# Scores of three more batches as plain float32 products, and fewer operations on GpSimd, in a fused attention and mixer kernel

## The chip, the cores and the metric

The kernel runs on one core of a Trainium2 chip. The metric is the device time of one execution in microseconds (us); lower is better. The engines are named as in the profile: PE (TensorE, matrix products), PEld (its weight loads), DVE (VectorE), ACT (ScalarE), POOL (GpSimd) and SP (SyncE, which issues all DMAs here).

## The reference, cut to what matters

```python
def _attn_ref(q, k, v):                      # 8 batches, 8 heads, 576 positions, 64 wide
    scores = np.matmul(q, k.transpose(0, 1, 3, 2)) / np.sqrt(64)
    scores = np.where(block_i >= block_j, scores, -1e9)      # blocks of 64 positions
    scores = scores - np.max(scores, axis=-1, keepdims=True)
    attn = np.exp(scores)
    attn = attn / (np.sum(attn, axis=-1, keepdims=True) + 1e-09)
    return np.matmul(attn, v)

def _moe_ref(x, w_theta, w_tok_r, w_tok_i, w_ch):            # x: 8 x 576 x 512
    theta = x @ w_theta
    zr, zi = x * np.cos(theta), x * np.sin(theta)
    y = np.einsum('ts,bsd->btd', w_tok_r, zr) + np.einsum('ts,bsd->btd', w_tok_i, zi)
    u = x + y
    return u + np.maximum(u @ w_ch, 0.0)
```

The output of the attention, with the heads side by side, is the x of the second function.

## The kernel before, in words

Every batch b has four pairs of heads, so that pairs p run from 0 to 31 and heads n from 0 to 63. A pair goes through these steps. q and k arrive by DMA, 128 rows (two heads of 64) by 640 columns. `scores` multiplies them in three pieces, "ab", "c" and (in `first_scores`) "d". `maxima` takes the row maxima on DVE, five pieces (L588), and `exponentials` takes exp on ACT out of PSUM into a tile t (L592). `high` writes 2^15 t in float16 (L314 to L320, a helper `times` that all such casts share), `low` on DVE writes what float16 lost (L619), a DMA transposes both (L623), `weighted` multiplies them with v on PE (L638), and `normalise` divides (L645 to L653).

When the four pairs of a batch are there, the mixer of that batch follows: `theta` (PE, L727) in five blocks of rows i = 0 to 4; `turns` (ACT, L737) and `rest` (DVE, L743) reduce the angle; `size` and `sines` (ACT, L749 to L763) give cosine and sine; `times_x` ("z", L773), `z_high` ("zh") and `z_low` ("zl", L786) make the operand and its two float16 parts; `mix` (PE, L796) sums over positions in steps n = 0 to 4, and step n needs the z parts of step n; `take_u` (L809), `u_high`, `u_low` (L820), `channel` (PE, L828) and `rectify` (L834) finish, and the result is stored. The x parts (`x_high`, `x_low`, L713), the sums `add_parts` ("xs", L801) and `unscale` ("xd") stand between the attention and the mixer.

A product of float32 numbers is made in two ways. In a *split* product each operand is cut into a high and a low part, and three fast products are summed: high with high, low with high, high with low. For the scores the parts are `q_high`, `q_low` (L519), `k_high` and `k_low` (L524) in the type float32r. In a *plain* product the float32 operands go to PE as they are. The constant `PLAIN = 4` says that pairs 0 to 3 take the plain way, in the scores and also in everything up to `weighted`: for them t is turned on PE (`turn_half`, L604) rather than by DMA.

Nothing in the kernel loops over time: all steps are put into one table of parts, each with what it needs, and `PLACES` gives the place of each part in one long order. Each engine, and SP's queue, runs its own steps in that order and no other, so that a step that waits holds up everything behind it on its engine. `BANKS` gives the PSUM bank of each result, `RUNNING` puts matmuls that compute nothing at some places (L1032), and `ON` says for each kind of step and each instance which engine runs it: P is POOL, D is DVE, A is ACT.

```python
products = [(hi, pair.v1), (hi, pair.v2), (lo, pair.v1)]                 # weighted, split
return (self.qh, self.kh), (self.ql, self.kh), (self.qh, self.kl)       # scores, split
return (self.qh, self.k),                                                # scores, plain
needs = [("mix", b, dt, th, n - 1)] if n else ...                        # order within mix
```

Of the kernel before, what the change touches and what calls it, by code (L numbers as in the profile page):

```python
# [180 lines left out]


RUNNING = [
    (12, 0, 7), (24, 0, 12), (41, 0, 8), (53, 0, 1), (74, 0, 2), (334, 7, 12), (354, 0, 3)
]
ON = {"w5": "APAAAAA",
      "wc": "DPPDDD",
      "vc": "PDPPDDPDPPPPDDDPDPPPDPPP",
      "qh": "PPPAPPPPPAAAPAAAAAPPPAAPAPPPAAPP",
      "vf": "PPPP",  # L190
      "cp": "AADDDAAADAADADDA",
# [14 lines left out]
PLAIN = 4  # L206
# [879 lines left out]
```

## Time and profile before

| | |
|---|---|
| median of 3 runs | 690.64 us (688.83 to 692.03) |
| the profiled execution, own time | 691.77 us |
| its span, first to last instruction | 690.0 us |
| busy: PE, PEld | 660.6 us (96%), 537.5 us (78%) |
| busy: DVE, ACT, POOL | 587.2 us (85%), 482.1 us (70%), 308.3 us (45%) |
| share of the span on the chain that ended last | PE 57%, DVE 20%, DMA 9%, ACT 8%, issue 4%, POOL 1% |

A busy share is a mean over stages with different limits. The chain that ended last follows the work back from the last instruction, each time to what released it. An engine's idle time counts only where that engine, or one that waits for it, sets the end. In a timeline, matmuls overlap, so the time that PE needs for a group is taken from the start of the group to the start of the next.

### The profile page before, as it was taken

How to read it: one execution, taken by the hardware profiler on the slowest of the kernel's cores; microseconds unless marked ns; L12 is line 12 of the kernel's file. 1: busy time of each engine (PE TensorE's matmuls, PEld its weight loads, DVE VectorE, ACT ScalarE, POOL GpSimd, SP SyncE). 2: the span in 40 equal slices, each digit the busy share in tenths (PEclk: the TensorE clock that was granted, in tenths of full speed). 3: DMA queues.
4: the chain of work that ended last, by engine and by line, in shares of the span. 5: the costliest groups of instructions: out<-in, count | busy, mean ns of one | idle time of the engine just before them, and what ended most of it. 6: DMA issues, size and time to landing. Idle time of an engine off the chain costs nothing.

```text
span 690.0 us, 17713 instructions
## 1 busy us (share of the span) xinstructions
PE 660.6 (96%) x7427; PEld 537.5 (78%) x7427; DVE 587.2 (85%) x846; ACT 482.1 (70%) x746; POOL 308.3 (45%) x280
## 2 busy tenths in 40 slices
PE   7998999999979999999999999999999999999997
PEld 4787866789657769887787768888797878888677
DVE  5897998998989999998979899999998999865342
ACT  4998699667896688877876598757867659613420
POOL 1513545422333734553653244674472673825640
PEclk9997999999989999999999999999999999999999
DMA  9971279699799888699866897969996875650001
GB/s 329 344 259 54 80 162 172 133 187 190 201 168 185 177 200 172 162 190 207 197 155 136 172 182 158 204 140 184 193 214 116 150 130 124 134 108 35 35 1 69
DMA packets 245855, 110.52 MB, mean 160 GB/s; under 512 B 227216, under 2 KB 227216, under 8 KB 245776
## 3 DMA queue, kind: packets, MB, share of 16 engines
q1 hardware_dynamic: 245776, 109.40, 71.5%
q8 instruction: 58, 0.95, 0.6%
q14 instruction: 21, 0.17, 0.1%
HBM read 43.06 MB, written 9.44 MB: 76 GB/s over the span
## 4 chain that ended last, share of the span: by engine, by line
PE 57%; DVE 20%; DMA 9%; ACT 8%; issue 4%; POOL 1%; SPq 0%; ACTq 0%; DVEq 0%; POOLq 0%
PE ps L796 20%; PE ps L828 11%; PE ps L727 10%; PE ps L638 8%; PE ps L554 7%; DVE m L588 4%; DMA pt<-p 3%; DVE p L619 3%; ACT t L592 2%; DMA q<-in_qT 2%; DVE zl L786 2%; DVE u_all L809 1%; ACT p L316 1%; DMA w_raw<-in_w_tok 1%; DMA raw_v<-in_v 1%
## 5 line engine op out<-in xcount | busy, mean ns | idle before, releaser
L592 ACT ACTIVATE t<-ps,m 128x576 f32<-128x576 f32 (+4 forms) x320 | 148.4, 528 | 59.1 <-DVE m L588 47.7
L796 PE MATMUL ps<-wT_h,zh 128*128 128x288 f16 x540 | 155.5, 288 | 5.9 <-ACT zh L314 3.0
L796 PE MATMUL ps<-wT_h,zl 128*128 128x288 f16 x540 | 155.2, 287 | 1.8 <-DVE zl L786 1.8
L796 PE MATMUL ps<-wT_l,zh 128*128 128x288 f16 x540 | 155.2, 287 | 0.0
L588 DVE TENSOR_REDUCE m<-ps 128x2 f32<-128x640 f32 (+4 forms) x160 | 125.7, 814 | 11.9 <-PE ps L559 9.7
L796 PEld LDWEIGHTS <-zh 128*128 128x128 f16 x1080 | 106.0, 98 | 30.9 <-ACT zh L314 3.1
L638 PE MATMUL ps<-v,pt 128*128 128x65 f16 (+1 forms) x2760 | 117.4, 202 | 7.0 <-DMA pt<-p 4.6
L619 DVE SCALAR_TENSOR_TENSOR p<-t,p 128x1664 f16<-128x1664 f32 x56 | 110.5, 1976 | 8.5 <-ACT p L316 7.2
L638 PEld LDWEIGHTS <-pt 128*128 128x128 f16 x2520 | 81.8, 97 | 10.8 <-DMA pt<-p 5.9
L727 PE MATMUL ps<-wth_h,xt 128*128 128x512 f16 (+1 forms) x384 | 87.6, 345 | 0.2 <-DVE xt L713 0.2
L727 PEld LDWEIGHTS <-xt 128*128 128x128 f16 (+1 forms) x576 | 45.9, 102 | 43.3 <-issue 1.6
L828 PE MATMUL ps<-uh,wch_h 128*128 128x288 f32 x256 | 78.5, 307 | 0.5 <-DVE u_all L834 0.4
L828 PE MATMUL ps<-ul,wch_h 128*128 128x288 f32 x256 | 75.6, 295 | 0.0
L828 PE MATMUL ps<-uh,wch_l 128*128 128x288 f32 x256 | 75.6, 295 | 0.0
L316 ACT ACTIVATE p<-t 128x1664 f16<-128x1664 f32 x47 | 74.6, 1590 | 1.0
L796 PEld LDWEIGHTS <-zl 128*128 128x128 f16 x540 | 53.1, 98 | 19.0 <-issue 3.0
L727 PE MATMUL ps<-wth_l,xt 128*128 128x512 f16 (+1 forms) x192 | 57.3, 343 | 0.0
L554 PE MATMUL ps<-kh,qh 64*128 64x288 f32 (+1 forms) x336 | 53.9, 312 | 1.9 <-ACT t L592 1.6
L828 PEld LDWEIGHTS ps<-uh,wch_h 128*128 128x128 f32 x256 | 48.1, 188 | 2.4 <-DVE u_all L834 1.0
L554 PE MATMUL ps<-kh,ql 64*128 64x288 f32 (+1 forms) x336 | 48.9, 284 | 0.0
L554 PE MATMUL ps<-kl,qh 64*128 64x288 f32 (+1 forms) x336 | 48.7, 283 | 0.0
L828 PEld LDWEIGHTS ps<-ul,wch_h 128*128 128x128 f32 x256 | 48.1, 188 | 0.1
(154 smaller groups left out, 1345.4 us busy)
## 6 DMA issues: line engine op xcount, KB each, us to landing
raw_v<-in_v SPq DMA_DIRECT2D x32, 384.0 KB, 4.4
q<-in_qT SPq DMA_DIRECT2D x32, 320.0 KB, 3.3
k<-in_kT SPq DMA_DIRECT2D x32, 320.0 KB, 3.5
out<-u_all SPq DMA_DIRECT2D x32, 288.0 KB, 2.2
w_raw<-in_w_tok SPq DMA_DIRECT2D x9, 576.0 KB, 5.8
w_raw<-in_w_theta SPq DMA_DIRECT2D x4, 512.0 KB, 7.5
w_raw<-in_w_ch SPq DMA_DIRECT2D x4, 512.0 KB, 4.9
pt<-p SPq DMA_TRANSPOSE x56, 6.2
```

The source lines that it names most:

```text
L316: engine.mul(to, x, scale)
L554: nc.tensor.matmul(s[hh][:, col:col + n], lhsT=qq[rows, i * P:(i + 1) * P], rhs=kk[rows, k0:k0 + n], start=nn == 0 and (j == 0 or c == "ab ...
L588: nc.vector.tensor_reduce(out=m, in_=s, axis=AX.XY if i in (2, 3) else AX.X, op=ALU.max, negate=True)
L592: nc.scalar.activation(out=to, in_=s, func=AF.Exp, scale=1.0, bias=m)
L619: nc.vector.scalar_tensor_tensor(out=self.p[:, 1, :], in0=self.t, scalar=LIFT, in1=self.p[:, 0, :], op0=ALU.mult, op1=ALU.subtract)
L638: nc.tensor.matmul(o[:, i, :], lhsT=pp[:, block, :], rhs=vv[:, of, hh, :], start=nn == 0, stop=nn == n - 1)
L727: nc.tensor.matmul(g[rows, 0:cols.stop - cols.start], lhsT=x[:, dt, part, i, rows], rhs=ww[:, dt, cols], start=(n == 0), stop=(n == 11))
L786: engine_of("zl", (2 * self.b + hf) * 5 + n).tensor_tensor(out=zl, in0=cv, in1=zh, op=ALU.subtract)
L796: nc.tensor.matmul(g, lhsT=zz[:, kk, cols], rhs=ww[:, kk, ts], start=(n == 0 and kk == k0 and nn == 0), stop=(n == 4 and nn == 2))
L809: nc.vector.scalar_tensor_tensor(out=self.u(dt)[:, ts], in0=bank("y", self.b, dt, th)[:, 0:HS], scalar=self.batch.unit, in1=self.u(dt)[:, ...
L828: nc.tensor.matmul(g[:, 0:HS], lhsT=ww[:, dt, e * P:(e + 1) * P], rhs=uu[:, dt, th * HS:(th + 1) * HS], start=(n == 0), stop=(n == 11))
```

## The change

`PLAIN` is split in two. A new `WHOLE = 4` keeps the old boundary for everything after the scores, and `PLAIN = 16` now governs the scores alone: pairs 4 to 15 (batches 1 to 3) have plain scores, their k goes by DMA straight to where PE reads it, and their steps `k_high`, `k_low` and `q_low` are gone. In `ON` the kinds v1, high, xh, xl, zh, kl, xs, xd and uh have no P any more. `PLACES`, `BANKS` and `RUNNING` are new throughout, as the list of parts is shorter (2570 for 2606); the filling matmuls are 45 in both.

```diff
-    3, 2, 17, 20, 23, 63, 101, 118, 8, 6, 34, 37, 39, 52, 102, 138, 27, 30, 72, 77, 79, 137, 228, 248, 47, 44, 85,
...
 RUNNING = [
-    (12, 0, 7), (24, 0, 12), (41, 0, 8), (53, 0, 1), (74, 0, 2), (334, 7, 12), (354, 0, 3)
+    (12, 0, 7), (25, 0, 13), (44, 0, 8), (64, 0, 3), (314, 0, 4), (370, 3, 5), (376, 3, 2), (386, 3, 3)
 ]
-      "kh": "DDDDPAPPAAPPAAPAPAAPPAAPPAPPAAPP",
-      "kl": "DDDDDPPPDDPDDPPDDDDPDDDDDPPPDPDP",
-      "v1": "DDDDPAPAPAPAAPAAAAAPAPPAAAAAAPAP",
-      "high": "DDDDDDDDAAPAAAAAAAAAAAAAAAAPAAAAAAAAPAAAAAAAPAAAAAAAPPAAAAPPAPAA",
-      "xh": "AAAAAAAAPDAAAADPAPADAAPPDPAPADPPAADPAPA",
-      "xl": "DDDDDPPDPDPDPDDDDPDDDDDPDPPDPDPPDPDDDDD",
-      "zh": "APDPPDAADPAPDDPADAPDADADDAPAAAAADAAAAAADAAAAPDDADAAPAADAPDAAPPAAADDAAPPDPAAPPDPA",
-      "xs": "DDDDPDDPDPDPPDPD",
-      "xd": "DAPPAAAADAAAPADA",
-      "uh": "AAAPAAAAAPAAAPAA",
+      "v1": "DDDDAAAAAAAAAAAAAAAAAAAAAAAAAAAA",
+      "high": "DDDDDDDDAAAAAAAAAAAAAAAAAAAAAAAAAAAAAAAAAAAAAAAAAAAAAAAAAAAAAAAA",
+      "kh": "DDDDDDDDDDDDDDDDAAPPAAPAAPPPAAPP",
+      "kl": "DDDDDDDDDDDDDDDDDDDDDDDDDDDDDDDD",
+      "xh": "AAAAAAAAADAAAADAAAADAAAADAAAADAAAADAAAA",
+      "xl": "DDDDDDDDDDDDDDDDDDDDDDDDDDDDDDDDDDDDDDD",
+      "zh": "AAAAAAAAAAAAAAAAAAAAAAAAAAAAAAAAAAAAAAAAAAAAAAAAAAAAAAAAAAAAAAAAAAAAAAAAAAAAAAAA",
+      "xs": "DDDDDDDDDDDDDDDD",
+      "xd": "DDDDAAADDAAADAAA",
+      "uh": "AAAAAAAAAAAAAAAA",
...
-PLAIN = 4
+WHOLE = 4
+PLAIN = 16
...
-            if pair.p < PLAIN:
+            if pair.p < WHOLE:
                 products = [(self.turned.rearrange("p a c q -> p (a c q)").bitcast(F32).rearrange("p (c q) -> p c q", q=P), pair.whole)]
...
-            if p < PLAIN:
+            if p < WHOLE:
                 free_pt = turn_of(f"pt{hh}", [("weighted", n)])
```

Three places show what moves. All line numbers of the changed kernel are one lower than before.

PE, the scores of pair 9 (batch 2), pieces "d" and "c", with the matmuls that add the mask. k and q are the operands, h and l their high and low parts. Before:

```order
L567 MATMUL ps<-kh,qh 128x64 x2
L567 MATMUL ps<-kh,ql 128x64 x2
L567 MATMUL ps<-kl,qh 128x64 x2
L554 MATMUL ps<-kh,qh 128x320 x2
L554 MATMUL ps<-kh,ql 128x320 x2
L554 MATMUL ps<-kl,qh 128x320 x2
L554 MATMUL ps<-kh,qh 128x192 x2
L554 MATMUL ps<-kh,ql 128x192 x2
L554 MATMUL ps<-kl,qh 128x192 x2
L559 LDWEIGHTS mask_q
```

And now:

```order
L566 MATMUL ps<-k,qh 128x64 x2
L553 MATMUL ps<-k,qh 128x320 x2
L553 MATMUL ps<-k,qh 128x192 x2
L558 LDWEIGHTS mask_q
L558 MATMUL ps<-ones,mask_q 128x2x64
```

One plain instruction stands where three stood; so for all three pieces of twelve pairs.

ACT, in the mixer of batch 1, from the sizes of the angles on (aa and rr hold angles, then cosine and sine; t and p belong to the attention of pairs 10 and 11). Before, up to the first zh:

```order
L749 ACTIVATE aa<-rr 128x1024 x2
L314 CAST xp<-x_ring 128x640
L761 ACT_TABLE_LOAD
L761 ACTIVATE aa<-aa,half_pi 128x1024
L763 ACTIVATE rr<-rr 128x1024
L761 ACTIVATE aa<-aa,half_pi 128x1024
L763 ACTIVATE rr<-rr 128x1024
L316 ACTIVATE p_98<-t_94 128x1664
L316 ACTIVATE v_86<-raw_v,sizes 128x12x64
L314 CAST zh<-aa 128x512
```

And now, up to the last of the batch's `turns`:

```order
L748 ACTIVATE aa<-rr 128x1024
L736 ACTIVATE aa<-ps,sizes 128x256
L313 CAST xp<-x_ring 128x640
L591 ACTIVATE t_93<-ps,m 128x64
L591 ACTIVATE t_94<-ps,m 128x64
L315 ACTIVATE p_97<-t_93 128x1664
L736 ACTIVATE aa<-ps,sizes 128x512
L748 ACTIVATE aa<-rr 128x256
L760 ACT_TABLE_LOAD
L760 ACTIVATE aa<-aa,half_pi 128x1024
L762 ACTIVATE rr<-rr 128x1024
L736 ACTIVATE aa<-ps,sizes 128x512
```

The cosine and sine of the first two blocks of rows now come before the last block's `turns` (L736 now, L737 before); before, they came after all five. On PE the order goes with it: before, the block i = 1 of theta was the last of the five, with 3 `weighted` and the scores of one pair, less its "d" piece, between it and the first mix step; now it is the second, with the other three theta blocks, 4 `weighted` and more scores in between.

POOL, in the same stretch. Before:

```order
L318 TENSOR_SCALAR u_all<-u_all,sizes 128x1152
L505 TENSOR_SCALAR qh<-q 128x640
L318 TENSOR_SCALAR u_all<-u_all,sizes 128x1152
L318 TENSOR_SCALAR v_85<-raw_v,sizes 128x12x64
L713 TENSOR_TENSOR xp<-x_ring,xp 128x640
L773 TENSOR_TENSOR rr<-rr,x_ring 128x2x2x128
L318 TENSOR_SCALAR zh<-rr 128x512
L773 TENSOR_TENSOR aa<-aa,x_ring 128x256
L318 TENSOR_SCALAR zh<-aa 128x256
L524 TENSOR_TENSOR kl<-k,kh 128x640
```

And now:

```order
L504 TENSOR_SCALAR qh<-q 128x640 x2
L772 TENSOR_TENSOR aa<-aa,x_ring 128x2x2x128
L772 TENSOR_TENSOR rr<-rr,x_ring 128x2x2x128
L772 TENSOR_TENSOR aa<-aa,x_ring 128x256
L785 TENSOR_TENSOR zl<-rr,zh 128x512
L772 TENSOR_TENSOR aa<-aa,x_ring 128x256
L772 TENSOR_TENSOR rr<-rr,x_ring 128x2x2x128
L785 TENSOR_TENSOR zl<-aa,zh 128x512
```

The casts (L318) and the low parts of x and k (L713, L524) have left POOL; z and zl stay with it, and q_high.

## Rows read from the trace of the kernel before

**Rows 1.** The page's first part: busy time, share, instructions of PE.

```profile
PE 660.6 (96%) x7427; PEld 537.5 (78%) x7427; DVE 587.2 (85%) x846; ACT 482.1 (70%) x746; POOL 308.3 (45%) x280
```

**Rows 2.** Busy time by stage; columns are in the first row.

```profile
core 0: us, PE busy (x) PEld busy (x) DVE busy (x) ACT busy (x) POOL busy (x), PEclk, DMA share, GB/s
0.00:75.00 75.00, 64.95 (x490) 53.78 (x491) 57.62 (x90) 58.94 (x97) 23.97 (x48) 0.93 0.66 231
75.00:190.00 115.00, 111.68 (x1312) 87.93 (x1312) 107.84 (x156) 90.46 (x142) 45.57 (x48) 1.00 0.79 166
190.00:220.00 30.00, 24.83 (x342) 19.96 (x342) 28.11 (x43) 24.42 (x35) 7.92 (x7) 0.89 0.99 175
220.00:400.00 180.00, 174.94 (x2174) 143.30 (x2174) 164.08 (x242) 135.08 (x210) 85.46 (x71) 1.00 0.83 177
```

**Rows 3.** Timeline of all engines, 194 to 199 us: start, us, engine, line.

```profile
194.27 1.55 PE L638 MATMUL ps<-v,pt 128*128 128x65 f16 x45 [1.84 <-DMA pt<-p]
...
198.19 0.60 ACT L314 CAST zh<-aa 128x512 f16<-128x512 f32 x1
...
198.84 0.42 PE L796 MATMUL ps<-wT_h,zh 128*128 128x288 f16 x1 [3.02 <-ACT zh L314]
```

**Rows 4.** Timeline of PE, plain scores of pair 0: pieces ab and c.

```profile
5.21 2.00 PE L554 MATMUL ps<-k,qh 64*128 64x288 f32 x16
7.04 0.22 PE L559 MATMUL ps<-ones,mask_q 64*128 64x128 bf16 x2
...
11.49 1.13 PE L554 MATMUL ps<-k,qh 64*128 64x320 f32 x8 [1.31 <-ACT t L592]
12.46 0.22 PE L559 MATMUL ps<-ones,mask_q 64*128 64x128 bf16 x2
```

**Rows 5.** Timeline of PE, split scores: piece c, then piece ab.

```profile
135.50 0.41 PE L554 MATMUL ps<-kh,qh 64*128 64x320 f32 x2
...
136.37 0.23 PE L559 MATMUL ps<-ones,mask_q 64*128 64x128 bf16 x2
...
142.04 0.40 PE L554 MATMUL ps<-kh,qh 64*128 64x288 f32 x2
...
143.60 0.23 PE L559 MATMUL ps<-ones,mask_q 64*128 64x128 bf16 x2
```

**Rows 6.** Groups of instructions by line and form: busy us, mean ns, idle before.

```profile
L619 DVE SCALAR_TENSOR_TENSOR p<-t,p 128x1664 f16<-128x1664 f32 x56 | 110.5, 1976 | 8.5 <-ACT p L316 7.2 <-POOL p L318 1.1
L316 ACT ACTIVATE p<-t 128x1664 f16<-128x1664 f32 x47 | 74.6, 1590 | 1.0
L519 DVE SCALAR_TENSOR_TENSOR ql<-q,qh 128x640 fp32r<-128x640 f32 x28 | 27.4, 979 | 1.4 <-ACT qh L503 1.4
L318 POOL TENSOR_SCALAR p<-t 128x1664 f16<-128x1664 f32 x9 | 20.1, 2232 | 24.1 <-DMA raw_v<-in_v 7.8 <-DMA pt<-p 7.3 <-ACT t L592 7.0
L773 DVE TENSOR_TENSOR rr<-rr,x_ring 128x512 f32<-128x512 f32 x19 | 17.0, 894 | 0.9 <-ACT rr L763 0.8
L801 DVE TENSOR_TENSOR u_all<-xt 128x1152 f32<-128x1152 f16 x10 | 16.6, 1673 | 1.0 <-DMA out<-u_all 0.9
L786 DVE TENSOR_TENSOR zl<-rr,zh 128x512 f16<-128x512 f32 x17 | 15.2, 897 | 0.3
L713 DVE TENSOR_TENSOR xp<-x_ring,xp 128x640 f16<-128x640 f32 x15 | 14.8, 984 | 1.7 <-ACT xp L314 0.9 <-POOL xp L318 0.8
L314 ACT CAST zh<-rr 128x512 f16<-128x512 f32 x13 | 8.0, 617 | 4.0 <-DVE rr L773 2.6 <-POOL rr L773 0.9 <-PE ps L796 0.3
L320 DVE TENSOR_SCALAR zh<-rr 128x512 f16<-128x512 f32 x9 | 6.9, 774 | 0.0
```

**Rows 7.** One line's instructions: duration in ns, least/median/most, first and last start.

```profile
L619 DVE SCALAR_TENSOR_TENSOR p<-t,p x56: 1845/1884/4308, 83.4 to 598.0; 128x1664 f16<-128x1664 f32 x56
L773 DVE TENSOR_TENSOR rr<-rr,x_ring x19: 654/692/1476, 106.9 to 634.5; 128x512 f32<-128x512 f32 x19
L519 DVE SCALAR_TENSOR_TENSOR ql<-q,qh x28: 807/818/2994, 44.8 to 568.8; 128x640 fp32r<-128x640 f32 x28
```

**Rows 8.** Busy time by stage, the stretch with ACT busiest.

```profile
100.00:130.00 30.00, 28.87 (x375) 21.86 (x372) 28.09 (x43) 27.62 (x40) 13.91 (x14) 1.00 0.76 148
```

More of the change, by code (lines that the diff above doesn't have):

```diff
@@ L32 @@
 PLACES = [
[134 rows of a table removed]
[132 rows of a table added]
 ]
 BANKS = [
[11 rows of a table removed]
[11 rows of a table added]
 ]
 RUNNING = [
-    (12, 0, 7), (24, 0, 12), (41, 0, 8), (53, 0, 1), (74, 0, 2), (334, 7, 12), (354, 0, 3)
+    (12, 0, 7), (25, 0, 13), (44, 0, 8), (64, 0, 3), (314, 0, 4), (370, 3, 5), (376, 3, 2), (386, 3, 3)
 ]
[L186 to L191, printed above, removed]
-      "n0": "DDAAADDAAADADDDDDDDDDADDDADADADDADADDDDDADDAAAADADDDDAAAAADAADAD",
-      "kh": "DDDDPAPPAAPPAAPAPAAPPAAPPAPPAAPP",
-      "kl": "DDDDDPPPDDPDDPPDDDDPDDDDDPPPDPDP",
-      "v1": "DDDDPAPAPAPAAPAAAAAPAPPAAAAAAPAP",
-      "high": "DDDDDDDDAAPAAAAAAAAAAAAAAAAPAAAAAAAAPAAAAAAAPAAAAAAAPPAAAAPPAPAA",
-      "xh": "AAAAAAAAPDAAAADPAPADAAPPDPAPADPPAADPAPA",
-      "xl": "DDDDDPPDPDPDPDDDDPDDDDDPDPPDPDPPDPDDDDD",
-      "z": "PDDDPPDDDDDDDPDDDDDPPDPPPPPDDDPPPPDDDPPPDDDPDPDPPPPPDDPDPDDPDDDPPDDDDDPDPPDPDDPP",
-      "zh": "APDPPDAADPAPDDPADAPDADADDAPAAAAADAAAAAADAAAAPDDADAAPAADAPDAAPPAAADDAAPPDPAAPPDPA",
-      "zl": "PDDDPPDPPDDDDDDPDPDDPPDPPDPPPDDPDDPDPDPPDDPDDPPPDPDPPDDPDDDDDDPPPDPDPDPDDDPPPPPP",
-      "xs": "DDDDPDDPDPDPPDPD",
-      "xd": "DAPPAAAADAAAPADA",
-      "uh": "AAAPAAAAAPAAAPAA",
-      "ul": "DPPDDPDDDDPPDPPD"}
-PLAIN = 4
+ON = {"w5": "AAAAAAA",
+      "wc": "DDDPPP",
+      "vc": "PPDPDDDDPPDDDPPDPDDPDPDD",
+      "qh": "APPPPPPPPAPPPPPPAAPPPPAAAAAPPPAP",
+      "vf": "PPDP",
+      "cp": "DADAADAAAADDDAAA",
+      "n0": "DDDAAAADDDDDDDDAAADADADAADAAAADAADDDAADDDDAADDADDDDADDDDDADDDAAA",
+      "v1": "DDDDAAAAAAAAAAAAAAAAAAAAAAAAAAAA",
[4 more added lines that the diff above has]
+      "xl": "DDDDDDDDDDDDDDDDDDDDDDDDDDDDDDDDDDDDDDD",
+      "z": "DDPDPPDPPPDDDPPPPDDPDDDDPDPPDDPPDDDDPDPPDDDPPPDPPDPDPDPPDDDDDDPDPDDDPPPPDPPPDDPP",
+      "zh": "AAAAAAAAAAAAAAAAAAAAAAAAAAAAAAAAAAAAAAAAAAAAAAAAAAAAAAAAAAAAAAAAAAAAAAAAAAAAAAAA",
+      "zl": "DPPPPPPPPDDPDDPPDPPDDPPDPDPPDPDDPDPDPDPPPDPPPDPPPPPPPPPPDDDPDPDPDDDPDDDDPDDDDPPP",
+      "xs": "DDDDDDDDDDDDDDDD",
+      "xd": "DDDDAAADDAAADAAA",
+      "uh": "AAAAAAAAAAAAAAAA",
+      "ul": "DDDPDPDPDPPPDPDP"}
+WHOLE = 4
+PLAIN = 16
 Part = namedtuple("Part", "f needs takes leaves")
@@ L291, in attention_phase_mixer @@
     for i in range(2):
-        count_keys(*([v_whole[i]] if i < PLAIN else v_parts[i]))
+        count_keys(*([v_whole[i]] if i < WHOLE else v_parts[i]))
     t = [const.tile([P, WIDE], F32, name=f"t{i}") for i in range(2)]
@@ L890, in attention_phase_mixer @@
             add(("k", p), pairs[p].load_k, turn_of("kr", [("kl", p)]) if p >= PLAIN else turn_of("kh", s_last, QK_BUFS))
-            add(("v", p), pairs[p].load_v, turn_of(f"raw_v{pr}", [("v2" if p >= PLAIN else "vf", p)]))
+            add(("v", p), pairs[p].load_v, turn_of(f"raw_v{pr}", [("v2" if p >= WHOLE else "vf", p)]))
             if pr % 2:
@@ L914, in attention_phase_mixer @@
         free = turn_of(f"v{p % 2}", [("weighted", n) for n in heads])
-        if p < PLAIN:
+        if p < WHOLE:
             add(("vf", p), pair.v_scaled, [("v", p), ("vc", b, 2)] + free)
-            if p >= PLAIN - 2:
+            if p >= WHOLE - 2:
                 add(("vo", p % 2), step_of(count_keys, *v_parts[p % 2]), turn_of(f"v{p % 2}", [("vo", p % 2)]))
@@ L930, in attention_phase_mixer @@
             add(("m", p, i), step_of(pair.maxima, i), needs + (free if i == 3 else [("m", p, 3)]))
-        free = [turn_of(f"t{hh}", [("low", n)] if p >= PLAIN else [("tp", n, half) for half in range(2)]) for hh, n in enumerate(heads)]
+        free = [turn_of(f"t{hh}", [("low", n)] if p >= WHOLE else [("tp", n, half) for half in range(2)]) for hh, n in enumerate(heads)]
         for hh, i in rows:
@@ L942, in attention_phase_mixer @@
             made = [("e", p, h_, i) for h_, i in rows if h_ == hh]
-            if p < PLAIN:
+            if p < WHOLE:
                 free_pt = turn_of(f"pt{hh}", [("weighted", n)])
@@ L954, in attention_phase_mixer @@
                 turned_by = [("turn", n)]
-            add(("weighted", n), h.weighted, turned_by + [("v2" if p >= PLAIN else "vf", p)] + turn_of("o", [("normalise", n, 2)]))
+            add(("weighted", n), h.weighted, turned_by + [("v2" if p >= WHOLE else "vf", p)] + turn_of("o", [("normalise", n, 2)]))
             needs = [("weighted", n)] + turn_of("r", [("normalise", n, 2)], 2)
```

287 rows, old and new, of tables (BANKS, PLACES) are left out of this document.

## The prediction

> **What bounds the kernel now.** I read the page first. PE is busy for 660.6 of 690.0 us [rows 1], so at most some 29 us of its span are empty, and no change to the other engines can give back more than that and what a low clock costs. Then the stages. PE stands idle for 75.0 - 64.95 = 10.05 us in the first 75 us, 115 - 111.68 = 3.3 from 75 to 190, 30 - 24.83 = 5.2 from 190 to 220 and 180 - 174.94 = 5.1 from 220 to 400 [rows 2]. That is 23.6 of the 29 us: after 400 us PE hardly waits. In the same rows DVE is busy for 107.84 of 115, 28.11 of 30 and 164.08 of 180 us, that is 94%, 94% and 91%. So up to 400 us two engines are nearly full, and a wait of PE is mostly a wait for something that DVE, or ACT behind DVE, delivers late. The granted clock is at full speed except for 0.93 in the first stage and 0.89 in 190 to 220 [rows 2], which is the 1.2 GHz level for about 0.11 x 30 x 2 = 6.6 us of that stage; it cost up to 0.11 x 30 = 3.3 us. The timeline shows what PE did ahead of it: 1.84 us without work for a transposed p, then 3.02 us for the zh of batch 1, which ACT cast only at 198.19 us [rows 3].
>
> **The change, part by part.**
>
> *Plain scores, on PE.* Measured from the start of a piece to its mask matmul, the plain piece ab takes 7.04 - 5.21 = 1.83 us and c 12.46 - 11.49 = 0.97 us [rows 4]. The split ones take 143.60 - 142.04 = 1.56 and 136.37 - 135.50 = 0.87 us [rows 5]. So plain costs 0.27 + 0.10 = 0.37 us more per pair; the small piece d I leave at nothing either way, since it is a twentieth of the columns. Twelve pairs: **+4.4 us** on the engine that is full, all of it on the path. As bounds I take 3.3 us, the pieces ab alone, and 4.9, a tenth more for d.
>
> The Trainium skill (FP8 and Floating Point Precision, TensorE Precision Notes) says that true FP32 takes four passes through the array. By that rule, against three fast products, this term would be an estimate of 9.7 us and the sum would end 5.3 us higher; the trace does not agree so far, with 17% more for ab and 11% for c where the rule has a third.
>
> *Steps that go.* Twelve each of k_high, k_low and q_low go. On DVE that is 12 q_low x 0.979 = 11.7 us [rows 6]; of k_low DVE runs sixteen before and after, so that those which go are POOL's in the count. DVE also gives up 20 zh casts, at most 0.774 each, some shorter, say 12 us, and seven zl x 0.897 = 6.3 us [rows 6].
>
> *Steps that come from POOL.* DVE takes 13 x_low x 0.984 = 12.8 us and 6 add_parts x 1.673 = 10.0 us [rows 6], and four unscale of the size of an add_parts with one input, which I put at 1 us each, at most 1.7. Net for DVE: -11.7 - 12 - 6.3 + 12.8 + 10.0 + 4 = -3 us. ACT takes 9 `high` x 1.590 = 14.3 us, 36 zh casts x 0.617 = 22 us, and 21 casts of x and v, not shorter than those, 13 us or more; it gives up nine casts of q and k, 5.6 us at the same price. Net for ACT: +44 us, from 482 to some 526.
>
> *What POOL's ops cost DVE.* The same instruction on DVE has very different durations. L619 takes 1845 ns at least and 1976 on average, 56 times, L773 654 against 894, 19 times, and L519 807 against 979, 28 times [rows 6, 7]. The excess is 7.3 + 4.6 + 4.8 = 16.7 us in three groups alone. They have two inputs in SBUF, and what runs beside them at their longest is POOL; 84 of POOL's 285 instructions go, the long ones (2.232 us for a `high`) among them. If excess follows count, 30% of 16.7 = 5 us comes back, the lower end; all of it is 16.7, the upper. I take 10, as the other two-input groups must have it too. So DVE is relieved by about 13 us, the most of it while the plain pairs run, where its share is highest.
>
> *What that is worth to PE.* A wait of PE is worth only its own length, so I go by stages:
> - 190 to 220 us: 5.2 idle and 3.3 of clock, together 8.5. In the new order the cosine and sine of rows 0 and 1 of batch 1 stand ahead of the last theta block, and PE has three theta blocks and more between its second theta block and the first mix, where it had three `weighted` and scores. I take **-7**; the wait for the transposed p may stay.
> - 75 to 190 and 220 to 400: 3.3 + 5.1 = 8.4 us idle, DVE at 91 to 94%. I take **-6**. Behind DVE the next to be late is the DMA of a transposed p, as in rows 3.
> - 0 to 75 us: 10 us idle and 0.07 x 75 = 5 us of clock. Here weights, q, k and v load and are cut, which the change hardly touches; pairs 4 and 5 lose their splits. I take **-1.5**. SP's queue moves too: k of a plain pair waits for the scores two pairs before it, where it waited for k_low of the pair before, and what stands behind it in SP's queue (v, transposes) waits along. I put it at nothing, since SP waited for k_low before.
> - After 400 us: nothing. The fillers are 45 in both and cost the same.
>
> **The sum** stands against the profiled execution's own 691.8 us, 1.1 above the median of 690.6: 691.8 + 4.4 - 7 - 6 - 1.5 = 681.7, and 1.1 less for a median, **680.6 us**.
>
> **The rivals.**
> 1. *DVE paces the whole first half.* If PE's waits up to 400 us are all DVE's lateness, both stage sums go whole (8.5 + 8.4) and half of the start's 15: 691.8 + 4.4 - 16.9 - 7.5 - 1.1 = 670.7 us. For it: 94% busy. Against: PE itself is at 97% in 75 to 190 us.
> 2. *No change.* The waits I remove come back at other places of an order that is wholly new, so that only about 4.4 us of them is gained, which the plain scores eat: 690.6 us. For it: 13.7 us of waits from 75 to 400 are already few.
> 3. *Slower: ACT becomes the bound.* It gets 44 us, which over the 500 us in which attention runs is 2.6 us per 30 us. In 100 to 130 us ACT is busy for 27.62 of 30 [rows 8]; with 2.6 more it would be 30.2, full. There exponentials and zh are late, and PE waits at each batch's first mix steps. It decides from where ACT has no idle time left between a batch's theta and its first mix. Price: one `high` of 1.59 us ahead of a zh, in seven batches, 11 us, with none of the gain: 691.8 + 4.4 + 11 - 1.1 = 706 us; with half of it, 699. Against: over the stages of rows 2 ACT is at 75 to 81%, and much of its wait is for DVE.
> 4. *Plain scores cost a third more than split ones* where PE is full on either side: (1.56 + 0.87) / 3 = 0.81 us a pair, 9.7 for twelve in place of 4.4, so 680.6 + 5.3 = 685.9 us, and more where a low clock meets them, so that I count it as no change. The rows speak against it, unless the loosely filled start, where they were read, hid something. The Trainium skill's four passes, cited above, would be the reason.
>
> **How the numbers follow.** About 0.5% (3.5 us) is what a measurement of this kernel tells from no change. Forecast (674 to 687 us): 0.45. Rival 1: 0.16. Rival 2: 0.18. Rival 3: 0.17, since three engines would stand within some per cent of full. Rival 4: 0.04, counted as no change. So faster 0.61, same 0.22, slower 0.17. The range takes in the forecast, rival 2, most of rival 1 and the nearer half of rival 3: 667 to 697 us.
>
> **What would show it.** Right: in the new profile PE is busy some 4 us more by its groups yet ends earlier; plain ab pieces last 1.83 us in the middle of the program as at its start; DVE's busy time is 565 to 580, its two-input means nearer to their least values; ACT some 526, POOL under 220; the clock shows full speed from 190 to 220 us. Wrong: ACT over 95% in some stage with PE waiting for L591 or zh there (rival 3); PE idle after 75 us of 13 us or more (rival 2); plain pieces of 2.1 us (rival 4); PE waiting for DMA of p or k where it waited for DVE.

## The result, and the profile after

The changed kernel takes **681.68 us** (median of 5 runs, 680.53 to 684.92) against 690.8 us of the kernel before in the same session: ratio 0.9863, 95% interval 0.9839 to 0.9887. Forecast was 680.6 us, in a range of 667 to 697. Its profiled execution took 681.88 us with a span of 680.1; line numbers are one lower than before. First the busy time of the engines from the page (span, then part 1), then by stage; they answer to [rows 1, 2].

```profile
span 680.1 us, 17318 instructions
...
PE 659.1 (97%) x7259; PEld 530.9 (78%) x7259; DVE 559.6 (82%) x829; ACT 520.9 (77%) x807; POOL 180.0 (26%) x196
```

```profile
core 0: us, PE busy (x) PEld busy (x) DVE busy (x) ACT busy (x) POOL busy (x), PEclk, DMA share, GB/s
0.00:75.00 75.00, 68.36 (x535) 56.00 (x537) 59.83 (x94) 61.19 (x101) 22.63 (x49) 1.00 0.66 236
75.00:190.00 115.00, 111.46 (x1257) 83.39 (x1257) 101.81 (x144) 95.96 (x153) 29.64 (x30) 1.00 0.88 179
190.00:220.00 30.00, 26.26 (x299) 21.01 (x300) 25.07 (x40) 23.84 (x38) 9.87 (x10) 0.89 0.81 159
220.00:400.00 180.00, 178.31 (x2141) 143.54 (x2139) 164.25 (x234) 148.83 (x230) 44.73 (x43) 1.00 0.85 180
```

The reader should set the two tables side by side, as idle time of PE and granted clock. From 0 to 75 us PE is idle for 75 - 68.36 = 6.6 us where it was 10.05, and the clock is full where it was 0.93. From 75 to 190 us nothing changed (3.5 against 3.3 us idle). From 190 to 220 us there are 3.7 us in place of 5.2, at the same clock of 0.89. From 220 to 400 us 1.7 in place of 5.1. So the largest piece was made at the start, where least was forecast, and the stage on which most was set gave little. The timeline of ACT, then of PE, in the start shows how; of the kernel before:

```profile
54.05 2.38 ACT L316 ACTIVATE wT_h<-w_val,size_tok 128x1152 f16<-128x1152 f32 x2
56.34 0.72 ACT L592 ACTIVATE t<-ps,m 128x576 f32<-128x576 f32 x1
56.97 1.25 ACT L459 ACTIVATE unused<-raw_v 128x1280 uint8<-128x1280 f32 x1
...
58.73 0.26 ACT L645 ACTIVATE r<-ps,small 128x5 f32<-128x5 f32 x1
```

```profile
58.89 0.44 PE L567 MATMUL ps<-k,qh 64*128 64x64 f32 x4 [2.13 <-ACT t L592]
60.45 6.63 PE L638 MATMUL ps<-v,pt 128*128 128x65 f32 x30 [1.12 <-DVE x_ring L653]
```

The same stretch of the kernel before by short stages (length, PE busy, clock, DMA):

```profile
56.00:62.00 6.00, 2.75 (x22) 0.80 0.00 0
62.00:70.00 8.00, 8.00 (x40) 0.51 0.15 42
```

And of the changed kernel, PE:

```profile
58.30 3.53 PE L637 MATMUL ps<-v,pt 128*128 128x65 f32 x30 [0.64 <-DVE x_ring L652]
...
66.02 2.23 PE L637 MATMUL ps<-v,pt 128*128 128x65 f32 x19
```

Before, ACT cast two weights and ran the count of batch 1's v ahead of pair 3's exponentials and of the first step of head 4's `normalise`. PE stood for 2.13 and 1.12 us, and then `weighted` 5 took 6.63 us where it now takes 3.53: from 62 to 70 us the granted clock was 0.51, the 1.2 GHz level. In the new order the count and most of these casts come earlier, and `weighted` 5 stands ahead of the small scores that waited. One wait of 0.64 us is left, and the clock stays at 2.4 GHz. The start of `weighted` 6 moves from 74.4 to 66.0 us. Of these 8.4 us some 2.2 are no gain: one piece ab of scores and four transposes that stood ahead of it now stand behind it, so that 6.2 are left. The last channel's end moves by 9.9 us.

### The profile page after: what moved, and what is told of

It is laid out like the page before. It is cut to its first block, busy times and chain, and to the rows that moved or that the text cites. A ratio compares the mean times of both kernels' runs of the same rounds, so it can differ in the third digit from the quotient of the medians.

```text
span 680.1 us, 17318 instructions
## 1 busy us (share of the span) xinstructions
PE 659.1 (97%) x7259; PEld 530.9 (78%) x7259; DVE 559.6 (82%) x829; ACT 520.9 (77%) x807; POOL 180.0 (26%) x196
## 4 chain that ended last, share of the span: by engine, by line
PE 77%; DMA 9%; ACT 8%; DVE 4%; issue 1%; POOL 1%; SPq 0%; ACTq 0%; POOLq 0%; DVEq 0%
PE ps L795 29%; PE ps L827 15%; PE ps L637 11%; PE ps L726 10%; PE ps L553 9%; DMA pt<-p 5%; ACT t L591 2%; DMA q<-in_qT 2%; DVE m L587 2%; PE ps L566 1%; DMA w_raw<-in_w_theta 1%; DMA xt<-xp 1%; DMA w_raw<-in_w_tok 1%; ACT wT_h L315 1%; ACT aa L736 1%
## 5 line engine op out<-in xcount | busy, mean ns | idle before, releaser
L591 ACT ACTIVATE t<-ps,m 128x320 f32<-128x320 f32 (+4 forms) x320 | 149.9, 530 | 51.4 <-DVE m L587 42.9
L587 DVE TENSOR_REDUCE m<-ps 128x2 f32<-128x640 f32 (+4 forms) x160 | 125.2, 816 | 20.8 <-PE ps L558 16.6
L637 PE MATMUL ps<-v,pt 128*128 128x65 f16 (+1 forms) x2760 | 115.4, 201 | 7.5 <-DVE x_ring L652 5.6
L618 DVE SCALAR_TENSOR_TENSOR p<-t,p 128x1664 f16<-128x1664 f32 x56 | 107.2, 1919 | 12.6 <-ACT p L315 12.4
L315 ACT ACTIVATE p<-t 128x1664 f16<-128x1664 f32 x56 | 88.8, 1593 | 6.8 <-DMA pt<-p 5.6
L637 PEld LDWEIGHTS <-pt 128*128 128x128 f16 x2520 | 83.4, 98 | 12.8 <-issue 6.7
L772 POOL TENSOR_TENSOR aa<-aa,x_ring 128x512 f32<-128x512 f32 (+1 forms) x26 | 30.6, 1188 | 92.8 <-ACT aa L760 49.5
L553 PE MATMUL ps<-k,qh 64*128 64x288 f32 (+3 forms) x384 | 51.7, 401 | 2.0 <-ACT t L591 0.8
L504 POOL TENSOR_SCALAR qh<-q 128x640 f32<-128x640 f32 (+1 forms) x22 | 19.7, 894 | 112.6 <-PE ps L566 46.5
```

The costliest lines, as they stand in the source:

```text
L315: engine.mul(to, x, scale)
L504: engine.tensor_scalar(out=out, in0=x, scalar1=scale, scalar2=0.0, op0=ALU.mult, op1=ALU.add)
L553: nc.tensor.matmul(s[hh][:, col:col + n], lhsT=qq[rows, i * P:(i + 1) * P], rhs=kk[rows, k0:k0 + n], start=nn == 0 and (j == 0 or c == "ab ...
L587: nc.vector.tensor_reduce(out=m, in_=s, axis=AX.XY if i in (2, 3) else AX.X, op=ALU.max, negate=True)
L591: nc.scalar.activation(out=to, in_=s, func=AF.Exp, scale=1.0, bias=m)
L618: nc.vector.scalar_tensor_tensor(out=self.p[:, 1, :], in0=self.t, scalar=LIFT, in1=self.p[:, 0, :], op0=ALU.mult, op1=ALU.subtract)
```

## The experiments

The trace leaves two readings. Theory S: the gain is the start's, a wait and the half clock behind it, and the rest about cancels. Rival D: DVE's relief pays, by plain scores or by the moves off GpSimd, and the start is a side effect. (Some expectations below give D's name to another rival; each says which.) Each kernel is generated from the changed one by its tables: the order of the steps, their banks, and the engines (`ON`). In the diffs of orders a line is one step with its arguments, and only the moved ones stand there. Times are medians, ratios are to the kernel before, run beside them (690.2 to 691.1 us).

**Plain scores alone** (old order, old engines).

```diff
-PLAIN = 4
+PLAIN = 16
```

> The order, the banks and the engines of before; only the scores of pairs 4 to 15 are plain, their 36 splits left out (each k load moves behind the scores that free its buffer). Theory S (the gain is made in the first 75 us, where the new order keeps PE from a wait at 56 to 60 us and the half clock behind it; the plain scores cost PE about 3 us and give it nothing): 687 to 694 us, the half clock from 59 to 70 us still there. Rival D (the gain is DVE's relief by 11.7 us of q_low): 680 to 685 us, with fewer PE waits from 75 to 400 us.

Measured: 696.02 us, ratio 1.0089 (1.0057 to 1.0120). The kernel is slower, 2 us above S's range. DVE's busy time fell from 587.2 to 569.5 us, and D's 680 to 685 us are far off. But the 4.9 us are not the price of plain scores alone, for the edit made a wait of its own in the start. Here are one row of ACT and two of PE; in the kernel before, the same piece ab starts at 49.89 us with no wait ahead of it, and has the clock at full speed.

```profile
50.04 1.12 ACT L396 ACTIVATE u_all<-w_raw 128x1024 f32<-128x1024 f32 x1 [2.16 <-DMA w_raw<-in_w_ch]
51.81 3.59 PE L553 MATMUL ps<-k,qh 64*128 64x288 f32 x16 [1.82 <-ACT pt L610]
55.18 0.33 PE L558 MATMUL ps<-ones,mask_q 64*128 64x128 bf16 x2
```

The load of pair 4's k now stands in SP's queue ahead of the loads of w_ch and waits 2.1 us there for scores; w_ch comes later, ACT waits for it, with the copies of the transposed p behind that, PE waits 1.82 us, and the clock from 50 to 56 us is 0.72. In the profiled execution `weighted` 4 starts 3.4 us later than in the kernel before, and the last channel ends 3.0 us later, so that behind this wait the plain scores together with DVE's relief cost nothing. What either is worth alone in the old order is not shown.

**Moves off GpSimd alone** (old order, split scores).

```diff
-      "high": "DDDDDDDDAAPAAAAAAAAAAAAAAAAPAAAAAAAAPAAAAAAAPAAAAAAAPPAAAAPPAPAA",
+      "high": "DDDDDDDDAAAAAAAAAAAAAAAAAAAAAAAAAAAAAAAAAAAAAAAAAAAAAAAAAAAAAAAA",
...
```

(The rows w5, v1, xh, xl, zh, xs, xd, uh and the last pairs of kl go the same way.)

> Before with the moves off GpSimd alone: order, banks and split scores as before. If DVE's relief from long GpSimd ops pays without anything else: 682 to 687 us. If ACT, with 44 us more, is late in an order that was not made for it: 692 to 702 us.

Measured: 710.58 us, ratio 1.0278 (1.0227 to 1.0328). GpSimd's busy time falls from 308.3 to 184.2 us, and the kernel is 20 us slower, so that D's other half fails in the old order too. Its waits of PE, the longest first (us in total, times, longest), and its timeline of ACT ahead of batch 1's first mix:

```profile
PE ps L797 <- ACT zh L315: 5.4, 1, 5.4
PE ps L639 <- DVE x_ring L654: 4.9, 5, 1.4
PE ps L568 <- ACT t L593: 2.8, 2, 2.2
```

```profile
202.17 1.57 ACT L317 ACTIVATE p<-t 128x1664 f16<-128x1664 f32 x1
203.65 0.60 ACT L315 CAST zh<-rr 128x512 f16<-128x512 f32 x1
204.16 0.93 ACT L317 ACTIVATE v<-raw_v,sizes 128x768 f16<-128x768 f32 x1
204.99 1.12 ACT L315 CAST zh<-aa 128x512 f16<-128x512 f32 x2
```

```profile
206.17 0.42 PE L797 MATMUL ps<-wT_h,zh 128*128 128x288 f16 x1 [5.39 <-ACT zh L315]
```

A `high` and a `v_first` stand on ACT ahead of a zh for which PE waits, which is the mechanism of the prediction's third rival. They stood there in the kernel before too, where the wait was 3.02 us [rows 3], so that this place gives 2.4 of the 20 us. The rest is spread over the program: the first mix starts 2.7 us later than before in batch 0, 7.3 in batch 1 and 18.3 in batch 7. Summed over the view, PE's waits for ACT grow from 10.9 to 16.6 us, and those for DVE from 6.2 to 17.2. That ACT alone paces this kernel is not shown; that the old order has no room for the moves is.

**Both, and the fourth corner.** First the moves with plain scores in the old order:

> The fourth corner of a square: the order and banks of before, with plain scores and the changed kernel's engines for all that left GpSimd. (The other corners: old order and old engines with plain scores 696.0 us, new order with old engines 709.2 us, both new 681.7 us.) If the moves are worth something of themselves, whatever the order: 684 to 690 us. If they only serve the order that was made with them: 694 to 705 us.

Measured: 713.93 us, ratio 1.0317 (1.0262 to 1.0372), 9 us worse than the worse forecast. Then the new order with the old engines:

```diff
-      "zh": "AAAAAAAAAAAAAAAAAAAAAAAAAAAAAAAAAAAAAAAAAAAAAAAAAAAAAAAAAAAAAAAAAAAAAAAAAAAAAAAA",
+      "zh": "APDPPDAADPAPDDPADAPDADADDAPAAAAADAAAAAADAAAAPDDADAAPAADAPDAAPPAAADDAAPPDPAAPPDPA",
...
```

> The changed kernel's order, banks and plain scores, but the engines of before for the ops that left GpSimd (high, x and z casts, x_low, v first parts, unscale and add, k_low of the last pairs). Theory S: DVE's relief is worth little, 680 to 685 us. Rival D: an order made for other engines waits at every place where GpSimd is slower, 690 us or more.

Measured: 709.17 us, ratio 1.0270 (1.0225 to 1.0316). With plain scores throughout, in us:

| | old engines | new engines |
|---|---|---|
| old order | 696.0 | 713.9 |
| new order | 709.2 | 681.7 |

S is refuted on this point, where it had 680 to 685 us. Neither has a worth of its own: the same moves cost 17.9 us in the old order and gain 27.5 in the new. "Order" takes in here what was made with it: the banks, the filling matmuls, and the engines of the kinds that the moves leave out (z_low, for one, is 46 times on GpSimd in place of 39). The upper left corner has the wait of its own that was shown above. In the new order with old engines `weighted` 6 still starts at 66.7 us (66.0 in the changed kernel, 74.4 before), so the start is the order's; but by 176 us, at theta of batch 1, that kernel is 2.2 us behind the one before.

**Split scores in the new order.**

```diff
-PLAIN = 16
+PLAIN = 4
...
 qh(p)
+kh(p)
+ql(p)
+kl(p)
```

> The changed kernel with split scores for pairs 4 to 15, the 36 splits on the engines of before, each as soon as its inputs are there; order otherwise and banks as in the changed kernel. If plain scores only cost PE their 3 to 4 us: 677 to 680 us. If the new order needs the room that they leave on DVE, ACT and GpSimd: 685 to 695 us.

Measured: 730.03 us, ratio 1.0559 (1.0484 to 1.0634), far beyond both. I had put the splits straight behind `q_high`, or, where k's buffer came free later, behind that, and nothing else gave way. Its waits of PE from 75 to 270 us:

```profile
PE ps L555 <- ACT t L593: 6.0, 2, 4.7
PE ps L639 <- DVE x_ring L654: 5.8, 3, 4.6
PE ps L728 <- DVE u_all L835: 5.1, 1, 5.1
```

All are waits for DVE or ACT, behind which the added steps stand; the clock is 0.94 in 75 to 190 us. Ahead of that PE waits 4.7 us for a step of GpSimd, and `weighted` 4 starts 7.0 us later than in the changed kernel. This shows that the new order has no room for 36 more steps there. It gives no price for plain scores: that a planned order with splits would do as badly is not shown.

**The start: the wait put back.**

```diff
-vz(1, 1)
 m(3, 3)
 sc(3)
+vz(1, 1)
+w(5, 5)
+w(7, 1)
 normalise(4, 0)
-w(7, 1)
 weighted(5)
-w(5, 5)
...
```

> The changed kernel with three ACT steps (v's count of the second batch, one weight cast, one exponent of weights) put ahead of head 4's normalise, so that weighted 5 waits at 58 us by some 3 us, as in the kernel before; all else as in the changed kernel. If the wait and a half clock behind it both cost their length to the end: 687 to 691 us. If the wait alone does: 684 to 686 us. If later slack takes it in: 681 to 683 us.

Measured: 688.33 us (685.32 to 694.95, 10 runs), ratio 0.9974 (0.9936 to 1.0012); its profiled execution took 688.38 us, 6.5 more than that of the changed kernel. Its PE, and its stages from 50 to 80 us (PE busy, clock):

```profile
61.42 6.13 PE L637 MATMUL ps<-v,pt 128*128 128x65 f32 x30 [2.73 <-DVE x_ring L652]
...
73.47 2.79 PE L637 MATMUL ps<-v,pt 128*128 128x65 f32 x24
```

```profile
56.00:62.00 6.00, 3.27 (x30) 1.00 0.00 0
62.00:70.00 8.00, 8.00 (x41) 0.50 0.10 19
70.00:80.00 10.00, 10.00 (x82) 0.89 0.29 91
```

This is the first of the three ranges, theory S's, and the fastest of the ten runs is slower than the slowest of the changed kernel's five (684.92). It is the cleanest run of all: three ACT steps moved, one wait of 2.73 us in place of 0.64, and the half clock returns. `weighted` 5 starts 3.1 us later and `weighted` 6 is 7.5 us later; 1.0 us of both was there at `weighted` 4, ahead of the wait. By `weighted` 21 some 1.1 us are taken in, and from there to the last channel the lag stays at 6.4 us. The longer wait is 2.1 us of the price, a third, and the half clock behind it most of the rest.

**The start mended in the kernel before.** Seven steps moved behind `weighted` 5, in the order of before:

```diff
-w(5, 5)
-w(4, 5)
-vz(1, 1)
-w(6, 5)
-w(2, 5)
 weighted(5)
+vz(1, 1)
 e(3, 1, 0)
+w(5, 5)
...
```

> Before with seven steps moved: four casts of weights and the three steps of the second batch's v count stand behind pair 3's exponentials and weighted 5 in place of ahead of them; nothing else. Theory S: the waits of 2.1 and 1.1 us at 56 to 60 us shrink, the clock stays at 2.4 GHz from 59 to 70 us, and the time falls by 4 to 8 us to 683 to 687 us. Rival D: the start is a matter of loads and casts that only come later, 689 to 692 us.

Measured: 689.08 us, ratio 0.9972 (0.9953 to 0.9991), in D's range and not in S's. The two waits shrank (`weighted` 5 starts 2.9 us earlier), but at 64.7 us PE met another one:

```profile
68.25 1.33 PE L605 MATMUL ps<-ident_r,t 128*128 128x128 f32 x5 [3.59 <-DVE pt L614]
```

DVE's copy of a transposed p stood behind low parts of weights, which waited for the casts that had been moved. So I moved those too:

```diff
 cp(7, 1)
+vc(1, -1)
+w(2, 5)
+w(5, 6)
+w(4, 6)
+w(6, 6)
...
```

> As the kernel with casts later, but v's count further behind and the low casts of weights behind the copies of transposed p, so that no copy waits for them on DVE. Theory S: neither the 2 us wait at 56 us nor the 3.6 us wait for a copy at 64 us, the clock at 2.4 GHz throughout the first 75 us: 683 to 686 us. Rival D: 689 to 692 us, the time goes to another wait ahead of the first mix.

Measured: 696.81 us, ratio 1.0098 (1.0062 to 1.0135), a miss on both sides. PE now waits 3.9 us for a size of the second batch's v count (L555 <- DVE sizes L353), which the move had made late. The casts have to be done before the transposed x of batch 0 overwrites their buffer, the count before batch 1's v: the wait moved from step to step.

**New start, old rest, and the reverse.**

```diff
-order: before, all steps
+order: after, up to weighted(6); then before's
```

> The steps up to weighted 6 in the order and on the engines of the changed kernel, all later ones in the order and on the engines of before, plain scores for pairs 4 to 15. Theory S: 8 us less than the kernel with plain scores alone, 680 to 685 us, with no half clock in the first 75 us. Rival D: within 2 us of the kernel with plain scores alone.

Measured: 693.55 us, ratio 1.0034 (1.0006 to 1.0062). Both ranges are missed. Where the two orders join, pair 4's small scores overwrite the bank of batch 0's first transposed x, so that it computes other numbers there, and PE waited for it. With the bank changed:

> As the kernel with the new start, but the transposed x of batch 0's first block sits in a bank that pair 4's small scores don't take (they waited 2.1 us for it, and the clock fell). Theory S: 6 to 9 us under the kernel with plain scores alone, 686 to 690 us. Rival D: within 3 us of it, 692 to 696 us.

Measured: 692.96 us, ratio 1.0040 (1.0015 to 1.0065), 3.1 us under plain scores alone (which lost some 3 us in their own start), less than S wanted and within D's range. `weighted` 6 starts 6.9 us earlier than in the kernel before, but then PE waits in the same way for another block of x, and the lead is gone:

```profile
76.90 0.43 PE L566 MATMUL ps<-k,qh 64*128 64x64 f32 x2 [2.10 <-DVE xt L712]
```

with a clock of 0.87 from 70 to 80 us. The other way round:

> The other way round: the steps up to weighted 6 in the order and on the engines of before, all later ones as in the changed kernel, plain scores for pairs 4 to 15. Theory S: the gain is lost, 687 to 692 us, with the half clock at 59 to 70 us. Rival D: the gain stays, 680 to 684 us.

Measured: 699.65 us, ratio 1.0122 (1.0078 to 1.0165). Here transposed x of blocks 2 and 4 of batch 0 share a bank, so that it too computes other numbers there. The gain is lost, as S says, but 8.6 us more with it, outside both ranges, at waits and half clocks that the join made (clock 0.74 from 70 to 100 us). Hybrids of two orders say little more than that their seams cost.

**The wait that is left, at 189 us.**

```diff
 weighted(19)
+z(1, 0, 0)
+normalise(19, 0)
+normalise(19, 1)
+normalise(19, 2)
 m(11, 2)
 zh(1, 0, 1)
+zh(1, 0, 0)
...
```

> The changed kernel with its longest remaining wait taken up: head 19's normalise on DVE and ahead of batch 1's maxima 2, 1 and 0 of pair 11 (ACT took its first step behind a sine), and z, zh and zl of batch 1's first block ahead of its fifth. If the 4.8 us wait ahead of weighted 20 at 189 us and the half clock behind it are worth their whole length: 676 to 679 us. If the first mix's operands are what ends last there (the wait goes to the mix, 2 to 3 us later): 680 to 682 us, no difference.

Measured: 682.49 us, ratio 0.9882 (0.9863 to 0.9902): no difference from the changed kernel. PE of the changed kernel at that place, then of this one:

```profile
193.74 2.63 PE L637 MATMUL ps<-v,pt 128*128 128x65 f16 x45 [4.75 <-DVE x_ring L652]
196.19 0.43 PE L795 MATMUL ps<-wT_h,zh 128*128 128x288 f16 x1
```

```profile
192.54 2.66 PE L637 MATMUL ps<-v,pt 128*128 128x65 f16 x45 [3.61 <-DMA pt<-p]
```

x_ring was ready at 190.15 instead of 193.59 us, and then the transposed p of head 20 ended last, at 192.5. Of 3.4 us that the mended step gave, 1.2 reached `weighted` 20 and none the end of batch 1's mix (237.4 us in both). They went at `weighted` 22, which had not waited before and now waits for its own transposed p; it starts at 216.33 us where it started at 216.40:

```profile
216.33 1.53 PE L637 MATMUL ps<-v,pt 128*128 128x65 f16 x45 [0.74 <-DMA pt<-p]
```

No version that was run beats the changed kernel.

## Why the prediction was right, and where its steps were not

**The total** (680.6 against 681.7 us) held, but by luck: two of its terms were in the wrong place, and their errors cancel. By stage, PE's idle time and clock, in us:

| step | forecast | measured |
|---|---|---|
| plain scores | +4.4 | about +2.5 by rows; the run by itself, +4.9, has a wait in its start that is not theirs |
| 190 to 220 us | -7 | -1.5 |
| 75 to 190 and 220 to 400 us | -6 | -3.2 (+0.2 and -3.4) |
| 0 to 75 us | -1.5 | -6 to -9 (`weighted` 6, like for like, -6.2; idle -3.4 and clock up to -5.2) |

*Plain scores.* Pieces ab and c cost what the start had shown. These are the changed kernel's rows in the middle of the program, then split pieces d, each read from its start to the start of what follows:

```profile
161.51 0.44 PE L566 MATMUL ps<-k,qh 64*128 64x64 f32 x4
161.78 1.08 PE L553 MATMUL ps<-k,qh 64*128 64x320 f32 x8
...
208.22 2.00 PE L553 MATMUL ps<-k,qh 64*128 64x288 f32 x16
210.06 0.22 PE L558 MATMUL ps<-ones,mask_q 64*128 64x128 bf16 x2
```

```profile
308.02 0.28 PE L566 MATMUL ps<-kh,qh 64*128 64x64 f32 x2
308.13 0.28 PE L566 MATMUL ps<-kh,ql 64*128 64x64 f32 x2
308.24 0.28 PE L566 MATMUL ps<-kl,qh 64*128 64x64 f32 x2
308.45 0.30 PE L795 MATMUL ps<-wT_h,zh 128*128 128x288 f16 x1
```

ab takes 210.06 - 208.22 = 1.84 us, as forecast. Piece d, left at nothing, takes 161.78 - 161.51 = 0.27 plain and 308.45 - 308.02 = 0.43 split, so plain is 0.16 cheaper there: 12 x (0.27 + 0.10 - 0.16) = 2.5 us. The step was mis-sized by 2 us, and its bounds (3.3 to 4.9) left out the gain on d. Rival 4 is refuted. The Trainium skill (FP8 and Floating Point Precision, TensorE Precision Notes) has four passes for true FP32; against three products that is a third more, where the trace has 17% more for ab and 37% less for d.

*DVE's relief.* The prediction said that "a wait of PE is mostly a wait for something that DVE, or ACT behind DVE, delivers late", and sized the stages by 13 us of relief. DVE was relieved by more, 27.6 us of busy time. But the run with plain scores alone relieved it by 17.7 us, and in its trace that paid, behind the start, for the 2.5 us that the plain scores cost and for 0.4 more, not for 13; the moves alone relieved it by 7.3 us and made the kernel 20 us slower, with PE's waits for DVE at 17.2 us. Relief is no gain by itself where the order stays: the steps that PE waits for must also stand earlier. That is the step that failed, and with it the -7, which measured -1.5: at 190 us it was taken that cosine and sine ahead of the last theta block would make zh early, but PE then waited 4.75 us ahead of `weighted` 20 instead, at the same half clock. "The wait for the transposed p may stay" proved true, as the run with head 19's normalise shows. What stood behind the DVE excess was sized fairly: L618 now takes 1853 ns at least and 1919 on average, an excess over the least of 56 x 0.066 = 3.7 us against 7.3 [rows 6, 7]; the first row gives least, median and most, the second busy time and mean.

```profile
L618 DVE SCALAR_TENSOR_TENSOR p<-t,p x56: 1853/1882/3858, 82.9 to 592.2; 128x1664 f16<-128x1664 f32 x56
```

```profile
L618 DVE SCALAR_TENSOR_TENSOR p<-t,p 128x1664 f16<-128x1664 f32 x56 | 107.2, 1919 | 12.6 <-ACT p L315 12.4
```

The excess halved while GpSimd's busy time fell from 308.3 to 180.0 us. By the Trainium skill (SBUF — State Buffer, SBUF: two separate sides) DVE with two inputs in SBUF and a GpSimd op that reads SBUF lock each other out; the row agrees in direction, and the run with the moves alone, where GpSimd is busy for 184.2 us and the kernel is slower, shows that this was not where the time was. (The prediction counts POOL's instructions as 285; the page has 280, and 84 of them are 30% either way.)

*The start.* "Weights, q, k and v load and are cut, which the change hardly touches" was wrong: it does not touch what is cut, but it moves when. [Rows 2] had the clue, a clock of 0.93 in that stage, and I priced the idle time and the clock there and then took a tenth of them. The run with the wait put back shows the price of that one place directly: 6.4 us in the profile, most of the 9 us in all. That it persists is shown by the same run. SP's queue, put at nothing, is nothing in the changed kernel, where ACT has no wait for w_ch; in the run with plain scores alone it made the wait of 1.82 us and a half clock.

*ACT.* Forecast some 526 us, measured 520.9; no stage of [rows 2] is over 85%, and PE waits nowhere long for zh. From 80 to 100 us, though, ACT is busy for 19.81 of 20 us, and PE waits 0.95 us for an exponential: the sign of rival 3, in one place and at a small price. As a whole rival 3 did not come true in this kernel; the run with the moves alone comes nearest to it, at 710.6 us, beyond its 699 to 706, with more of its added waits for DVE than for ACT. That rival's chance of 0.17 hung on the order, which the prediction had not weighed as a condition. Two signs of being right failed: the clock from 190 to 220 us, and PE's busy time, which fell by 1.5 us where it was to rise by 4 (`weighted` 5, at full speed, is busy for 3.1 us less). Rival 1 (670.7 us) fell with DVE's relief. Rival 2's mechanism, waits that come back at other places, was true of the stage from 190 to 220 us, but not of the start.

*Open.* How much the plain scores are worth to a new order can't be read here, since the run that took them back had no planned place for the splits; nor to the old one, since the run that put them in made a wait elsewhere. The reverse of the wait put back was not reached: no run took the wait out of the old order without making another. Nor was it tried which of the many moved steps after 75 us keep the start's gain; that they must go with the engine moves is shown by the corner at 709.2 us.

## What to carry to other kernels

Price a wait of TensorE early in the program with the half clock that follows it, and look for it where the mean clock of a stage is under 1.00, before looking at busy shares. An order written for one division of engines and the division itself are one thing: parts of such a change, tried one by one, can each lose 5 to 20 us while the whole gains 9. Before such a part's time is taken for its price, look in its trace for a wait that the edit made elsewhere. Where a wait is mended, ask what was due just behind it: here a transfer was, 1.2 us earlier than the wait that hid it.

## What the runs showed of the hardware that was not expected

A wait of 2.73 us ahead of `weighted` 5, or two of 2.13 and 1.12 us, was followed by a granted clock of 0.50 and 0.51 from 62 to 70 us; after a wait of 0.64 us in the same place it stayed at full speed. With plain scores alone, a wait of 1.82 us at 50 us went with a clock of 0.72 from 50 to 56 us: the piece ab behind it took 3.37 us to its mask matmul, where it takes 1.83 at full speed. A few us of waiting so cost as much again and more: a wait longer by 2.1 us made `weighted` 6 later by 6.4. Plain float32 scores of 64 columns were faster than three products of split ones (0.27 against 0.43 us), those of 288 columns slower (1.84 against 1.56 us).
